# Gate/up products in another Strassen order with three PSUM copies, wide weight sums, and W_down sums one pair later

## The chip, the cores and the metric

The kernel runs on one core of a Trainium2 chip. The metric is the device time of one execution in microseconds (us); lower is better. Times are medians of several executions. A profile of one execution gives the span from the first to the last instruction, about 1.7 us shorter than the time. Runs are compared in the fast state only (granted TensorE clock near 1.00). Engines: PE is TensorE, PEld its weight loads, DVE VectorE, ACT ScalarE, POOL GpSimd, SP the engine whose queue issues the DMA transfers.

## The reference, cut to what matters

A transformer block on x of 2048 x 1024: linear attention (part A), then a gated MLP (part B). The change lies in part B.

```python
h  = x + _A_ref(_layernorm(x), A_wqkv, A_wo)
h2 = h + _B_ref(_layernorm(h), B_W_gate, B_W_up, B_W_down)

def _B_ref(x, W_gate, W_up, W_down):          # W_gate, W_up: 1024 x 3584, W_down: 3584 x 1024
    gate = x @ W_gate
    up   = x @ W_up
    gate = gate * (gate > 0)                  # ReLU
    return (gate * up) @ W_down
```

## The kernel before

Tokens go in two passes of 1024. In each pass 14 *pairs* compute gate and up for two blocks of 128 features, and then a down stage multiplies by W_down. All these products use a Strassen-Winograd scheme: seven products P1 to P7 in place of eight. It needs sums of weight blocks (T1 to T4), sums of activation blocks (S1 to S4, once a pass), sums of W_down blocks (once, in pass 0, kept in DRAM), and combinations of the products:

```text
U1 = P1+P6   C11 = P1+P2   C12 = U1+P5+P3   C22 = U1+P7+P5   C21 = U1+P7+P4 (signs inside the sums)
```

Each engine executes its own list in order. A helper turns the buffers that an operation reads and writes into semaphore waits, so an operation that waits for its data holds everything behind it on that engine:

```python
def emit(self, e, eng):
    for op in self.prog[e]:          # program order
        waits = {}                   # ... semaphores of the operations it depends on ...
        ins = op.fn(eng)
        ins._wait_ge(last[0], last[1])
```

One pair before the change (w = 0 is gate, w = 1 is up; BA, BF_, BB, BC_ are two PSUM banks each; `fillin(n)` puts n T sums for the next pair into the DVE list; `mid` are the W_down sums):

```python
for w in range(2):
    prod(w, BA[w], w_blk(w, 0, 0), a_blk(0, 0), True, "P1")
    ident_act(bank(BB[w]), bank(BA[w]), ..., "fk1")           # ACT: PSUM -> PSUM
fillin(2)
for w in range(2):
    prod(w, BF_[w], t_blk(w, 2), s_blk(2), True, "P7")
    ident_act(ftmp[:, w, :], bank(BF_[w]), ..., "s7")
fillin(2)
for w in range(2):
    prod(w, BB[w], t_blk(w, 1), s_blk(1), False, "P6")
    ident_act(bank(BC_[w]), bank(BB[w]), ..., "fk2")
fillin(2)
for f_ in mid:
    f_()                                                      # DVE: W_down sums
for w in range(2):
    prod(w, BA[w], w_blk(w, 1, 0), a_blk(1, 0), False, "P2")
    ...                                                       # rl11 on ACT after gate
# DVE: hh11 = BA[1] * r11
fillin(2)
for w in range(2):
    prod(w, BC_[w], t_blk(w, 0), s_blk(0), False, "P5")
    ident_act(ftmp[:, 2 + w, :], bank(BC_[w]), ..., "sc")
    # DVE: c22 = BF_[w] + ftmp[2 + w]
for w in range(2):
    prod(w, BB[w], t_blk(w, 3), a_blk(1, 1), False, "P4")
    # DVE: c21 = BB[w] + ftmp[w];  after gate also hh22 = max(c22 gate, 0) * c22 up
for w in range(2):
    prod(w, BC_[w], w_blk(w, 1, 1), s_blk(3), False, "P3")
    # after gate: rl12 on ACT, hh21 on DVE
# DVE: hh12 = BC_[1] * r12
load_w_next(); load_w_next()
```

One W_down pair's sums are four DVE subtractions that first need 512 KB of W_down:

```python
def wd_sums(q):
    add(0, wb(0, 1), wb(0, 0), [B_wraw[k]])       # waits until W_down of pair q has landed
    add(2, wb(1, 1), wb(0, 1), [B_wraw[k]])
    add(1, wb(1, 1), wsum[:, k, 0, :], ...)
    add(3, wb(1, 0), wsum[:, k, 1, :], ...)
    ...                                           # next load, store of the sums
```

And around the pairs:

```python
load_w_next()                                     # gate and up weights, 512 KB each
load_w_next()
for q in range(NWR):
    load_wraw(q)                                  # W_down, 512 KB each
wt_at = {0: [0], 1: [1, 2], 2: [3, 4]}            # pair -> W_down sums in it
for q in range(3, 12):
    wt_at[q] = [q + 2]
```

## Time and profile before

| what | value |
|---|---|
| time | 747.1 us (745.5 to 748.2, four runs) |
| span in the profile | 744.1 us |
| busy: PE, DVE, ACT | 98%, 72%, 42% |
| granted clock | 1.00 |

From the page of the kernel before: busy us by engine (share of the span, instructions), then the shares of the chain of work that ended last.

```profile
PE 731.3 (98%) x3914; PEld 330.4 (44%) x3975; DVE 534.4 (72%) x1064; ACT 316.2 (42%) x558; POOL 42.4 (6%) x93
...
PE 85%; DVE 7%; issue 3%; DMA 2%; ACT 2%; SPq 1%; POOL 0%; DVEq 0%; ACTq 0%
```

A matmul of 512 columns is shown as busy 379 ns, but matmuls overlap, so "98% busy" does not say that PE runs at its rate. Counting does. The view by windows gives busy us and, in brackets, instructions of each engine in stretches of time:

```profile
core 0: us, PE busy (x) PEld busy (x) DVE busy (x) ACT busy (x) POOL busy (x), PEclk, DMA share, GB/s
244.00:250.00 6.00, 5.27 (x23) 1.77 (x22) 5.93 (x12) 2.05 (x5) 0.00 (x0) 1.00 0.81 242
250.00:262.00 12.00, 11.95 (x56) 5.48 (x56) 11.76 (x28) 5.95 (x12) 0.00 (x0) 1.00 0.78 235
...
520.00:532.00 12.00, 11.95 (x56) 5.47 (x56) 8.63 (x19) 5.82 (x11) 0.00 (x0) 1.00 0.33 89
```

A pair has 56 matmuls, and 56 in 12 us is one per 0.214 us: that is the rate. From 244 to 250 us only 22 or 23 started where 28 would fit: PE waited there. DVE is nearly full in the early pairs (11.76 of 12 us) and has over a quarter of its time free in a late one (8.63).

The rate shows best in the start times of the weight loads, since there is one per matmul: the median spacing is 0.216 us. After 231 us only four spacings in the whole trace are over 0.26 us, all between 244.7 and 249.2 us. The first pair of pass 0 (pair 0) has its loads from 231.22 to 243.3 us.

The timeline of the kernel before around there (start, duration, engine, line, operation, output<-input, count; in brackets idle time just before and what ended it). L581 are the W_down sums, L1161 T sums, L1230 hh11, L1237 c22:

```profile
234.53 0.71 SPq L501 DMA_DIRECT2D RWG<-in_B_W_up_dram  x1
...
235.35 9.20 SPq L501 DMA_DIRECT2D RW<-in_B_W_down_dram  x3
...
237.56 0.76 DVE L1161 TENSOR_TENSOR RO<-RWG 128x512 f16<-128x512 bf16 x2 [1.84 <-DMA RWG<-in_B_W_up_dram]
...
242.55 1.56 DVE L581 TENSOR_TENSOR RW<-RW 128x512 f16<-128x512 bf16 x4 [4.23 <-issue]
...
244.03 0.68 DVE L1230 TENSOR_TENSOR RAB<-ps,RAB 128x512 bf16<-128x512 f32 x1
...
244.77 1.04 PE L595 MATMUL ps<-RH,RWG 128*128 128x512 bf16 x4 [0.22 <-DVE RAB L1230]
...
246.16 2.85 PE L595 MATMUL ps<-RC,RO 128*128 128x512 f16 x12 [0.35 <-DVE RE L1237]
```

DVE stood still for 4.23 us in front of the W_down sums, until 242.55. "issue" only says that the profile recorded no event that ended the wait. The view of the transfers into RW between 228 and 246 us fills this in:

```profile
DMA to landing us min/median/max: 3.9/5.7/7.1
```

The longest of these took 7.1 us. It was the first W_down request, of 235.35 us: the landing events kept in the packed trace put its landing at 242.47 us, 0.08 us before the sums began. hh11 started at 244.03, 7.4 us after the first matmul of P2 (236.61). Below, "lost in pair 0" means what the late DVE work of pair 0 cost, also where PE met it only in pair 1.

### The profile page before, as it was taken

How to read it: one execution, taken by the hardware profiler on the slowest of the kernel's cores; microseconds unless marked ns; L12 is line 12 of the kernel's file. 1: busy time of each engine (PE TensorE's matmuls, PEld its weight loads, DVE VectorE, ACT ScalarE, POOL GpSimd, SP SyncE). 2: the span in 40 equal slices, each digit the busy share in tenths (PEclk: the TensorE clock that was granted, in tenths of full speed). 3: DMA queues.
4: the chain of work that ended last, by engine and by line, in shares of the span. 5: the costliest groups of instructions: out<-in, count | busy, mean ns of one | idle time of the engine just before them, and what ended most of it. 6: DMA issues, size and time to landing. Idle time of an engine off the chain costs nothing.

```text
span 744.1 us, 10780 instructions
## 1 busy us (share of the span) xinstructions
PE 731.3 (98%) x3914; PEld 330.4 (44%) x3975; DVE 534.4 (72%) x1064; ACT 316.2 (42%) x558; POOL 42.4 (6%) x93
## 2 busy tenths in 40 slices
PE   8999999999999999999999999999999999999998
PEld 3444444344444444444444444444444444444443
DVE  7978877798775999787876495766767767563343
ACT  4887667764922354454543100045445454520000
POOL 1311100001350000000000010000000000000000
PEclk9999999999999999999999999999999999999999
DMA  9644144024999787555528899742424242036664
GB/s 314 195 102 70 32 139 156 1 30 87 216 225 286 223 258 222 171 169 170 142 87 261 225 286 280 246 118 69 113 57 113 58 114 56 1 86 185 211 193 133
DMA packets 160228, 113.43 MB, mean 152 GB/s; under 512 B 51504, under 2 KB 141360, under 8 KB 160176
## 3 DMA queue, kind: packets, MB, share of 16 engines
q1 hardware_dynamic: 159504, 112.09, 54.8%
q8 instruction: 31, 0.51, 0.3%
q10 hardware_dynamic: 672, 0.66, 0.3%
q14 instruction: 21, 0.17, 0.1%
HBM read 85.46 MB, written 15.73 MB: 136 GB/s over the span
## 4 chain that ended last, share of the span: by engine, by line
PE 85%; DVE 7%; issue 3%; DMA 2%; ACT 2%; SPq 1%; POOL 0%; DVEq 0%; ACTq 0%
PE ps L595 85%; SPq L501 1%; DVE RAB L681 1%; DMA RE<-in_A_x_dram 1%; DVE RE L1056 1%; DVE RX L678 1%; DMA RAB<-RXH 1%; DVE RX L897 1%; ACT RX L674 1%; ACT RXH L633 0%; DVE RWG L816 0%; DMA RW<-in_B_W_down_dram 0%; DVE RW L791 0%; ACT ps L600 0%; DVE RXH L1080 0%
## 5 line engine op out<-in xcount | busy, mean ns | idle before, releaser
L600 ACT ACTIVATE ps<-ps 128x512 f32<-128x512 f32 x156 | 90.8, 583 | 169.8 <-PE ps L595 151.2
L595 PE MATMUL ps<-RC,RO 128*128 128x512 f16 x672 | 154.4, 379 | 0.5 <-DVE RE L1237 0.4
L595 PE MATMUL ps<-RW,RAB 128*128 128x512 f16 (+1 forms) x686 | 151.3, 379 | 0.5
L595 PE MATMUL ps<-RH,RWG 128*128 128x512 bf16 x448 | 106.0, 379 | 0.2 <-DVE RAB L1230 0.2
L595 PEld LDWEIGHTS ps<-RW,RAB 128*128 128x128 bf16 (+1 forms) x696 | 68.1, 98 | 82.1
L600 ACT ACTIVATE RE<-ps 128x512 f32<-128x512 f32 x120 | 70.8, 597 | 75.3 <-PE ps L595 52.8
L595 PEld LDWEIGHTS ps<-RC,RO 128*128 128x128 f16 x672 | 65.5, 98 | 80.5 <-ACT ps L600 1.1
L595 PE MATMUL ps<-RC,RWG 128*128 128x512 f16 x320 | 76.8, 379 | 0.4 <-ACT ps L600 0.4
L595 PEld LDWEIGHTS ps<-RH,RWG 128*128 128x128 bf16 x448 | 43.8, 98 | 53.3 <-DVE RAB L1230 0.7
L1230 DVE TENSOR_TENSOR RAB<-ps,RAB 128x512 bf16<-128x512 f32 x28 | 19.3, 690 | 63.5 <-PE ps L595 63.5
L600 ACT ACTIVATE RAB<-ps 128x512 bf16<-128x512 f32 x56 | 33.4, 597 | 61.9 <-PE ps L595 61.8
L595 PE MATMUL ps<-RW,RE 128*128 128x512 bf16 x243 | 56.6, 380 | 1.6 <-DVE RXH L1080 0.7
L595 PE MATMUL ps<-RH,RO 128*128 128x512 bf16 (+1 forms) x228 | 55.5, 379 | 1.5
L595 PEld LDWEIGHTS ps<-RC,RWG 128*128 128x128 bf16 (+1 forms) x320 | 30.0, 98 | 40.2 <-ACT ps L600 6.2
L1161 DVE TENSOR_TENSOR RO<-RWG,RO 128x512 f16<-128x512 bf16 x108 | 45.4, 421 | 1.8
L1161 DVE TENSOR_TENSOR RO<-RWG 128x512 f16<-128x512 bf16 x108 | 40.7, 418 | 3.1 <-DMA RWG<-in_B_W_up_dram 1.8
L595 PE MATMUL ps<-RAB 128*128 128x512 bf16 x172 | 42.5, 379 | 0.3
L1237 DVE TENSOR_TENSOR RE<-ps,RE 128x512 f32<-128x512 f32 x56 | 38.3, 690 | 4.8 <-ACT RE L600 4.8
L1242 DVE TENSOR_TENSOR RE<-ps,RE 128x512 f32<-128x512 f32 x56 | 38.2, 682 | 0.0
L595 PEld LDWEIGHTS ps<-RH,RO 128*128 128x128 f16 (+1 forms) x256 | 24.4, 98 | 30.1 <-ACT RX L600 1.6
L595 PEld LDWEIGHTS ps<-RW,RE 128*128 128x128 bf16 x256 | 24.0, 98 | 28.8 <-DVE RXH L1080 1.2
L609 DVE BATCH_NORM_STATS2 st<-RE 128x6 f32<-128x512 bf16 x34 | 22.1, 683 | 16.4 <-DMA RE<-h_scr 12.5
(108 smaller groups left out, 756.0 us busy)
## 6 DMA issues: line engine op xcount, KB each, us to landing
RWG<-in_B_W_gate_dram SPq DMA_DIRECT2D x28, 512.0 KB, 4.1
RWG<-in_B_W_up_dram SPq DMA_DIRECT2D x28, 512.0 KB, 5.1
RW<-t_scr SPq DMA_DIRECT2D x56, 256.0 KB, 3.3
RW<-in_B_W_down_dram SPq DMA_DIRECT2D x42, 256.0 KB, 4.5
RW<-in_B_W_down_dram SPq DMA_DIRECT2D x14, 512.0 KB, 4.0
t_scr<-RW SPq DMA_DIRECT2D x14, 512.0 KB, 5.0
RE<-in_A_x_dram SPq DMA_DIRECT2D x23, 256.0 KB, 3.6
h_scr<-RXH SPq DMA_DIRECT2D x16, 256.0 KB, 3.4
```

The lines of the kernel that those rows point to most:

```text
L501: return PL.add(eng, lambda e: e.dma_start(dst_ap, src_ap), reads=reads, writes=writes, slot=slot, name=name)
L595: lambda e: e.matmul(out_ap, lhsT, rhs, start=start, stop=stop, skip_group_check=skip),
L600: PL.add("act", lambda e: e.activation(out=dst, in_=src, func=func), reads=reads, writes=writes, name=name)
L609: PL.add("dve", lambda e: e.bn_stats(out=st6[:, k, c * 6:(c + 1) * 6], in_=src_full[:, c * BCH:(c + 1) * BCH]), reads=[src_chunk_bufs[c]], ...
L674: PL.add("act", lambda e: e.activation(out=Et[:, k, :], in_=src, func=ACTF.Exp), reads=[src_buf], writes=[B_E[k]], name=name + "_exp")
L678: PL.add("dve", lambda e: e.tensor_scalar(out=Et[:, k, :], in0=Et[:, k, :], scalar1=1.0, scalar2=1e-6, op0=ALU.min, op1=ALU.add), reads=[] ...
L681: PL.add("dve", lambda e: e.scalar_tensor_tensor(out=dst_ap, in0=src, scalar=C1, in1=Et[:, k, :], op0=ALU.add, op1=ALU.max), reads=[src_bu ...
L897: PL.add("dve", lambda e: e.tensor_tensor(out=s_, in0=p_, in1=s_, op=ALU.add), reads=[pb], writes=[sb_], name=name + "_add")
L1161: PL.add(eng, lambda e: e.tensor_tensor(out=Tring[:, k, j], in0=in0, in1=in1, op=ALU.subtract), reads=reads, writes=[B_T[k][j]], name="T%d ...
L1230: PL.add("dve", lambda e: e.tensor_tensor(out=hh[:, f1, 0:SBW], in0=bank(BA[1]), in1=r11[:, rr, :], op=ALU.mult), reads=[B_bank[BA[1]], B_ ...
L1237: PL.add("dve", lambda e, w=w: e.tensor_tensor(out=ftmp[:, 4 + w, :], in0=bank(BF_[w]), in1=ftmp[:, 2 + w, :], op=ALU.add), reads=[B_bank[ ...
L1242: PL.add("dve", lambda e, w=w: e.tensor_tensor(out=ftmp[:, 6 + w, :], in0=bank(BB[w]), in1=ftmp[:, w, :], op=ALU.add), reads=[B_bank[BB[w] ...
```

## The change

Its intent: less DVE work per pair, no early stop of DVE. There are three parts.

1. The order becomes P1 P5 P6 P2 P7 P3 P4. P5 is copied once to SBUF (s5) and added in on DVE for both c22 and c12; U1+P7 stays in one bank and P4 is added on top of it. Three PSUM copies by ACT per matrix (fk1, s5, fk2) replace four; two Relus come in. c22 and c12 are bf16, so two of the four last products read SBUF only.
2. A T sum is made for gate and up in one operation of 128x1024 (POOL's first ones stay narrow).
3. The W_down sums start in pair 1.

(The order in which the T sums and the S sums are made changes a little, too; the cut below leaves that out.)

```diff
             for w in range(2):
                 prod(w, BA[w], w_blk(w, 0, 0), a_blk(0, 0), True, "P1")
                 ident_act(bank(BB[w]), bank(BA[w]), [B_bank[BA[w]]], [B_bank[BB[w]]], "fk1")
-            fillin(2)
+            fillin(1)
             for w in range(2):
-                prod(w, BF_[w], t_blk(w, 2), s_blk(2), True, "P7")
-                ident_act(ftmp[:, w, :], bank(BF_[w]), [B_bank[BF_[w]]], [B_s7[w]], "s7")
-            fillin(2)
+                prod(w, BE[w], t_blk(w, 0), s_blk(0), True, "P5")
+                ident_act(ftmp[:, w, :], bank(BE[w]), [B_bank[BE[w]]], [B_s5[w]], "s5")
+            fillin(1)
   ... P6 with fk2, mid, P2 with rl11, hh11 as before ...
             for w in range(2):
-                prod(w, BC_[w], t_blk(w, 0), s_blk(0), False, "P5")
-                ... sc copy, c22 add, then P4 with the c21 add, then P3 ...
+                prod(w, BB[w], t_blk(w, 2), s_blk(2), False, "P7")
+                add_s5(c22[:, w, :], bank(BB[w]), B_bank[BB[w]], w, B_c22[w], "c22")
+            relu(c22[:, 0, :], c22[:, 0, :], [], B_c22[0], "rl22")
+            for w in range(2):
+                prod(w, BC_[w], w_blk(w, 1, 1), s_blk(3), False, "P3")
+                add_s5(c12[:, w, :], bank(BC_[w]), B_bank[BC_[w]], w, B_c12[w], "c12")
+                if w == 0:
+                    mul(hh[:, f2, SBW:2 * SBW], c22[:, 0, :], c22[:, 1, :], B_c22, B_hh[f2][1], "hh22")
+            relu(c12[:, 0, :], c12[:, 0, :], [], B_c12[0], "rl12")
             for w in range(2):
                 prod(w, BB[w], t_blk(w, 3), a_blk(1, 1), False, "P4")
+                if w == 0:
+                    relu(r12[:, rr, :], bank(BB[0]), [B_bank[BB[0]]], B_r12[rr], "rl21")
+            mul(... c12 gate, c12 up ..., "hh12")
+            mul(... bank(BB[1]), r12 ..., "hh21")
   ... t_sums: the same subtractions with one more dimension, gate and up ...
-        wt_at = {0: [0], 1: [1, 2], 2: [3, 4]}
-        for q in range(3, 12):
+        wt_at = {1: [0, 1], 2: [2, 3], 3: [4, 5]}
+        for q in range(4, 12):
             wt_at[q] = [q + 2]
```

More of the change, by code (lines that the diff above doesn't have):

```diff
@@ L268, in bass_sequential_preLN__linear_attn_block__glu_gated_reglu__prompt_kernel @@
         ftmp = RE[:, 0:(NO + NOT) * D].bitcast(f32).rearrange("p (a b) -> p a b", b=SBW)
+        c22 = RE[:, 2 * D:4 * D].rearrange("p (a b) -> p a b", b=D)[:, :, 0:SBW]
+        c12 = RE[:, 4 * D:6 * D].rearrange("p (a b) -> p a b", b=D)[:, :, 0:SBW]
         o0 = (NO + NOT) * D
@@ L402, in bass_sequential_preLN__linear_attn_block__glu_gated_reglu__prompt_kernel @@
         B_f = bufs("f_", 8)
-        B_s7, B_sc, B_c22, B_c21 = B_f[0:2], B_f[2:4], B_f[4:6], B_f[6:8]
+        B_s5, B_c22, B_c12 = B_f[0:2], B_f[2:4], B_f[4:6]
         B_U, B_V = B_f[0:4], B_f[4:8]
@@ L1146, in s_sums @@
             return [
-                lambda: add(2, blk(0, 0), blk(0, 1), ALU.subtract, bl(0) + bl(1)),
                 lambda: add(0, blk(0, 1), blk(1, 1), ALU.add, bl(1)),
                 lambda: add(1, Ssum[:, 0], blk(0, 0), ALU.subtract, [B_S[0]] + bl(0)),
+                lambda: add(2, blk(0, 0), blk(0, 1), ALU.subtract, bl(0) + bl(1)),
                 lambda: add(3, blk(1, 0), Ssum[:, 1], ALU.subtract, [B_S[1]] + bl(0)),
@@ L1155, in t_sums, with wb, tb, add @@
             k = L % NTR
-            def wb(kk, h):
-                return wring[:, i, kk * KH:(kk + 1) * KH, h * P:(h + 1) * P]
-            def add(j, in0, in1, reads):
-                PL.add(eng, lambda e: e.tensor_tensor(out=Tring[:, k, j], in0=in0, in1=in1, op=ALU.subtract),
-                       reads=reads, writes=[B_T[k][j]], name="T%d_%d" % (j + 1, L))
-            return [
-                lambda: add(0, wb(0, 1), wb(0, 0), [B_w[i]]),
-                lambda: add(2, wb(1, 1), wb(0, 1), [B_w[i]]),
-                lambda: add(1, wb(1, 1), Tring[:, k, 0], [B_w[i], B_T[k][0]]),
-                lambda: add(3, wb(1, 0), Tring[:, k, 1], [B_w[i], B_T[k][1]]),
-            ]
+            n = 1 if eng == "pool" else 2
+            def wb(kk, h, u):
+                return wring[:, i + u:i + u + n, kk * KH:(kk + 1) * KH, h * P:(h + 1) * P]
+            def tb(j, u):
+                return Tring[:, k + u:k + u + n, j]
+            def add(j, f0, f1, td):
+                def go(u):
+                    r = range(u, u + n)
+                    PL.add(eng, lambda e: e.tensor_tensor(out=tb(j, u), in0=f0(u), in1=f1(u), op=ALU.subtract),
+                           reads=[B_w[i + x] for x in r] + ([B_T[k + x][td] for x in r] if td is not None else []),
+                           writes=[B_T[k + x][j] for x in r], name="T%d_%d" % (j + 1, L))
+                return [lambda u=u: go(u) for u in range(0, 2, n)]
+            return (add(0, lambda u: wb(0, 1, u), lambda u: wb(0, 0, u), None) +
+                    add(1, lambda u: wb(1, 1, u), lambda u: tb(0, u), 0) +
+                    add(2, lambda u: wb(1, 1, u), lambda u: wb(0, 1, u), None) +
+                    add(3, lambda u: wb(1, 0, u), lambda u: tb(1, u), 1))
         def hh_sums(q):
@@ L1185, in strassen_pair @@
             kt = [l % NTR for l in L]
-            BA, BF_, BB, BC_ = [0, 1], [2, 3], [4, 5], [6, 7]
+            BA, BE, BB, BC_ = [0, 1], [2, 3], [4, 5], [6, 7]
             rr = q % 2
@@ L1210, in prod, with add_s5, mul, relu @@
                        "%s%s_%d_%d" % (name, "gu"[w], ps_, q), skip=True)
+            def add_s5(dst, src, bsrc, w, bdst, name):
+                PL.add("dve", lambda e: e.tensor_tensor(out=dst, in0=src, in1=ftmp[:, w, :], op=ALU.add),
+                       reads=[bsrc, B_s5[w]], writes=[bdst], name=name)
+            def mul(dst, a_, b_, reads, wr, name):
+                PL.add("dve", lambda e: e.tensor_tensor(out=dst, in0=a_, in1=b_, op=ALU.mult), reads=reads,
+                       writes=[wr], name=name)
+            def relu(dst, src, reads, wr, name):
+                ident_act(dst, src, reads, [wr], name, func=ACTF.Relu)
             for w in range(2):
@@ L1222, in strassen_pair @@
                 ident_act(bank(BC_[w]), bank(BB[w]), [B_bank[BB[w]]], [B_bank[BC_[w]]], "fk2")
-            fillin(2)
+            fillin(1)
             for f_ in mid:
@@ L1228, in strassen_pair @@
                 if w == 0:
-                    ident_act(r11[:, rr, :], bank(BA[0]), [B_bank[BA[0]]], [B_r11[rr]], "rl11", func=ACTF.Relu)
-            PL.add("dve", lambda e: e.tensor_tensor(out=hh[:, f1, 0:SBW], in0=bank(BA[1]), in1=r11[:, rr, :],
-                                                    op=ALU.mult),
-                   reads=[B_bank[BA[1]], B_r11[rr]], writes=[B_hh[f1][0]], name="hh11")
-            fillin(2)
-            for w in range(2):
-                prod(w, BC_[w], t_blk(w, 0), s_blk(0), False, "P5")
-                ident_act(ftmp[:, 2 + w, :], bank(BC_[w]), [B_bank[BC_[w]]], [B_sc[w]], "sc")
-                PL.add("dve", lambda e, w=w: e.tensor_tensor(out=ftmp[:, 4 + w, :], in0=bank(BF_[w]),
-                                                             in1=ftmp[:, 2 + w, :], op=ALU.add),
-                       reads=[B_bank[BF_[w]], B_sc[w]], writes=[B_c22[w]], name="c22")
+                    relu(r11[:, rr, :], bank(BA[0]), [B_bank[BA[0]]], B_r11[rr], "rl11")
@@ new lines, in strassen_pair @@
+            mul(hh[:, f1, 0:SBW], bank(BA[1]), r11[:, rr, :], [B_bank[BA[1]], B_r11[rr]], B_hh[f1][0], "hh11")
+            fillin(1)
+            for w in range(2):
+                prod(w, BB[w], t_blk(w, 2), s_blk(2), False, "P7")
[6 more added lines that the diff above has]
+                    mul(hh[:, f2, SBW:2 * SBW], c22[:, 0, :], c22[:, 1, :], B_c22, B_hh[f2][1], "hh22")
@@ L1240, in strassen_pair @@
+            relu(c12[:, 0, :], c12[:, 0, :], [], B_c12[0], "rl12")
             for w in range(2):
                 prod(w, BB[w], t_blk(w, 3), a_blk(1, 1), False, "P4")
-                PL.add("dve", lambda e, w=w: e.tensor_tensor(out=ftmp[:, 6 + w, :], in0=bank(BB[w]),
-                                                             in1=ftmp[:, w, :], op=ALU.add),
-                       reads=[B_bank[BB[w]], B_s7[w]], writes=[B_c21[w]], name="c21")
                 if w == 0:
-                    PL.add("dve", lambda e: e.scalar_tensor_tensor(
-                        out=hh[:, f2, SBW:2 * SBW], in0=ftmp[:, 4, :], scalar=0.0, in1=ftmp[:, 5, :],
-                        op0=ALU.max, op1=ALU.mult), reads=B_c22, writes=[B_hh[f2][1]], name="hh22")
@@ L1249, in strassen_pair @@
-            for w in range(2):
-                prod(w, BC_[w], w_blk(w, 1, 1), s_blk(3), False, "P3")
-                if w == 0:
-                    ident_act(r12[:, rr, :], bank(BC_[0]), [B_bank[BC_[0]]], [B_r12[rr]], "rl12", func=ACTF.Relu)
-                    PL.add("dve", lambda e: e.scalar_tensor_tensor(
-                        out=hh[:, f1, SBW:2 * SBW], in0=ftmp[:, 6, :], scalar=0.0, in1=ftmp[:, 7, :],
-                        op0=ALU.max, op1=ALU.mult), reads=B_c21, writes=[B_hh[f1][1]], name="hh21")
@@ L1256, in strassen_pair @@
-            PL.add("dve", lambda e: e.tensor_tensor(out=hh[:, f2, 0:SBW], in0=bank(BC_[1]), in1=r12[:, rr, :],
-                                                    op=ALU.mult),
-                   reads=[B_bank[BC_[1]], B_r12[rr]], writes=[B_hh[f2][0]], name="hh12")
+                    relu(r12[:, rr, :], bank(BB[0]), [B_bank[BB[0]]], B_r12[rr], "rl21")
+            mul(hh[:, f2, 0:SBW], c12[:, 0, :], c12[:, 1, :], B_c12, B_hh[f2][0], "hh12")
+            mul(hh[:, f1, SBW:2 * SBW], bank(BB[1]), r12[:, rr, :], [B_bank[BB[1]], B_r12[rr]], B_hh[f1][1], "hh21")
@@ L1560, in bass_sequential_preLN__linear_attn_block__glu_gated_reglu__prompt_kernel @@
         LAG = NOT
-        pool_t = t_sums(0, "pool") + t_sums(1, "pool")
+        pool_t = t_sums(0, "pool")
         for t in range(NE, NST + LAG + 1):
@@ L1590, in bass_sequential_preLN__linear_attn_block__glu_gated_reglu__prompt_kernel @@
                 if nxt < NPASS * NPAIR * 2:
-                    fill = fill + t_sums(nxt) + t_sums(nxt + 1)
+                    fill = fill + t_sums(nxt)
                 if q > 0:
```

## The prediction

> **What bounds the kernel.** TensorE. The page gives PE busy 98%; the 20 us windows are the better test: from 250 us to the end 92 to 94 matmuls start in each, one per 0.215 us, at granted clock 1.00. The Trainium skill ("VectorE: DVE Perf Modes", section on the TRN2 errata) gives 215 ns for a 512-column matmul; the trace agrees (median spacing of weight loads 0.216 us). So gate/up and down run at the matmul rate. A gate/up pair is 56 matmuls; the chain of waits shows pairs as unbroken 12.03 us pieces of PE. DVE (72%) and ACT (42%) hide under that: DVE is busy 8.6 to 10 of 12 us in an ordinary pair, 11.8 in the three pairs with two W_down sums.
>
> After 225 us the weight loads show only four gaps, all in the first gate/up pair: 0.60, 0.73, 0.29, 0.53 us at 244.8, 246.2, 248.0, 249.2, together 2.15 us. The timeline says why: DVE executes in order, and the W_down sums of pair 0 (L581) wait 4.2 us, until 242.55, for W_down, requested at 235.35. hh11, T sums and c22 stand behind them, and TensorE waits for the banks they read.
>
> **What the change does.**
> - Matmuls: same number, order P1 P5 P6 P2 P7 P3 P4. No PE time saved.
> - ACT: still ten 0.6 us ops per pair (sc copies go, two Relus come). Neutral.
> - DVE: eight T sums of 0.42 us become four of 128x1024 at about 0.69 us (other sums of that size here: 0.682 to 0.692): minus 0.6 us per pair. hh22 and hh12 become bf16 SBUF products, about 0.42 instead of 0.69 us: minus 0.5. Ordinary pair: about 9.7 to 8.6 us. With two W_down sums (3.1 us): 11.7 of 12.03.
> - W_down sums start in pair 1, when their data have long landed.
>
> **On the critical path.** Almost only the 2.15 us. The saved DVE time, about 31 us over 28 pairs, lies under a saturated TensorE and buys nothing. The wide T sums of pair 0 wait for gate and up together; up landed at 237.5. Then T1 to T3 end at 239.6, hh11 at 240.3, T4 at 241.0, the c22 adds at 241.7 and 242.4, and P4, which overwrites those banks, is due at 241.75 and 242.6: pair 0 just fits, or leaves some tenths of a us. Later c22 ends about 1.2 us before P4 needs its bank, and hh21 ends 0.8 us into the next pair, whose copy into that bank starts at 1.8. No new stall in steady state. The stages before 220 us (some 20 us of small PE gaps) are untouched.
>
> Estimate: minus 2.15 plus 0.3 left over, so 745.8 us, 0.25% faster. Range 744.3 to 747.5. Faster by over 2%: 0.5%; within 2%: 98.5%; slower: 1%.
>
> **What would show it.** Right: span near 742; gaps at 244 to 249 gone or below 0.5 us; DVE busy down by about 30 us, its share 67 to 68%; T sums x108 of about 690 ns; matmuls per 20 us unchanged; no idle before the W_down sums. Wrong: PE waits on DVE or ACT (c22, c12, Relu in place, fk1) repeated in each pair, pairs longer than 12.03 us in the chain; wide sums well above 0.7 us.
>
> **What would make it wrong.** A repeated wait I mis-ordered (0.1 us per pair would be 2.8 us); the three W_down pairs, where DVE has 0.3 us to spare, turning a late load into gaps of 1 to 2 us; a lower granted clock. A gain over 2% (15 us) has no source: TensorE's whole idle in these stages is 2.15 us.

## The result, and the profile after

The changed kernel took 744.52 us (744.17 to 744.85, four runs) against 747.1 us. The ratio is 0.997, 95% interval 0.9956 to 0.9984: within 2%, and a small real gain. Here and below a ratio is the mean time of one kernel's fast runs over that of the other's of the same rounds, so not quite the ratio of the medians quoted.

From the page of the changed kernel, the lines that answer to those above:

```profile
PE 731.5 (98%) x3914; PEld 331.3 (45%) x3975; DVE 514.0 (69%) x956; ACT 318.7 (43%) x558; POOL 42.1 (6%) x93
...
PE 88%; DVE 7%; ACT 2%; issue 2%; DMA 1%; POOL 1%; DVEq 0%; ACTq 0%
```

The same windows of the changed kernel:

```profile
244.00:250.00 6.00, 6.00 (x30) 2.74 (x28) 5.38 (x12) 3.66 (x7) 0.00 (x0) 1.00 0.56 144
250.00:262.00 12.00, 11.95 (x57) 5.40 (x56) 11.22 (x25) 5.98 (x10) 0.00 (x0) 1.00 0.85 264
...
520.00:532.00 12.00, 11.95 (x57) 5.40 (x57) 7.89 (x15) 5.98 (x10) 0.00 (x0) 1.00 0.32 90
```

The stretch from 244 to 250 us now holds its 28 weight loads. In the late pair PE does what it did before, while DVE has 0.74 us less to do. The chain in order of time, from 225 us, is PE alone, in pieces of 12.03 us (a pair's length) with 0.05 us "issue" between them. In pair 0 of before it ran over W_down and DVE (the first two lines below are of the kernel before, the rest of the changed one):

```profile
238.32 4.23 issue
242.55 1.11 DVE RW L581 x3
...
230.26 12.03 PE ps L597 x55
242.29 0.05 issue
242.35 12.03 PE ps L597 x55
```

The timeline of the changed kernel in pair 0 (L1169 T sums, L1225 products, L1221 c22 and c12, L583 W_down sums):

```profile
237.97 0.69 DVE L1169 TENSOR_TENSOR RO<-RWG 128x1024 f16<-128x1024 bf16 x1 [4.72 <-DMA RWG<-in_B_W_up_dram]
...
239.91 0.68 DVE L1225 TENSOR_TENSOR RAB<-ps,RAB 128x512 bf16<-128x512 f32 x1
...
241.11 1.88 DVE L1221 TENSOR_TENSOR RE<-ps,RE 128x512 bf16<-128x512 f32 x3
...
242.35 1.67 PE L597 MATMUL ps<-RH,RO 128*128 128x512 bf16 x7
...
248.23 3.02 DVE L583 TENSOR_TENSOR RW<-RW 128x512 f16<-128x512 bf16 x8
```

DVE still waits 4.72 us in pair 0, now for the up weights alone, and is done just in time: the first c22 add ends near 241.8 us and the weight load of P4, which adds to the bank that it reads, is at 241.92 (of its eight matmuls the trace holds seven, from 242.35). The W_down sums at 248.23 wait for nothing.

**How much PE time was lost.** A gap in the weight loads is not quite lost time: PE loads weights ahead of its matmuls (in pair 0 the first load starts at 231.22 us, the first matmul at 231.43), and after a stop this lead is gone (244.76 and 244.77), so each gap is about 0.2 us longer than the time lost. The whole loss is read by aligning the two traces by the number of the weight load (3975 in both) and following the difference of their start times. From load 1640, in pair 0, to the last, the changed kernel takes 503.75 us. The kernel before takes 505.10: 1.34 us more, all in the first products of pair 1. The same measure of every fast trace follows; the column of loads 1560 to 1640 is a stretch at the end of the attention stage and the start of pair 0, where the kernels differ little (the order of some sums and loads):

```text
kernel          load 1640 to last   lost in pair 0*  lost in loads 1560-1640   lost later
before               505.10              1.34                0.00                0.00
before_again         505.45              1.70                0.90                0.00
changed              503.75              0.00                0.00                0.00
after_again          503.76              0.00                0.00                0.00
wd_late              503.75              0.00                0.00                0.00
wd_late_again        503.75              0.00                0.50                0.00
wd_load_first        503.76              0.00                0.00                0.00
wd_early             510.95              7.19                0.00                0.00
dve_double           504.94              1.19                0.00                0.00
lag_old              503.76              0.00                0.00                0.00
lag_new              505.82              0.00                1.05                2.06
after_slack          503.75              0.00                0.73                0.00
```

("lost" is against the trace of the changed kernel. * In the two traces of the kernel before it fell in pair 1, see above; in the others in P4 of pair 0.) Five hundred microseconds at 0.216 us per load leave nothing to gain after 235 us at this rate: no trace here took less than 503.75 us for this number of matmuls.

### The profile page after: what moved, and what is told of

The parts are those of the page before. It is cut to its first block, busy times and chain, and to the rows that moved or that the text cites. A ratio compares the mean times of both kernels' runs of the same rounds, so it can differ in the third digit from the quotient of the medians.

```text
span 743.1 us, 10650 instructions
## 1 busy us (share of the span) xinstructions
PE 731.5 (98%) x3914; PEld 331.3 (45%) x3975; DVE 514.0 (69%) x956; ACT 318.7 (43%) x558; POOL 42.1 (6%) x93
## 4 chain that ended last, share of the span: by engine, by line
PE 88%; DVE 7%; ACT 2%; issue 2%; DMA 1%; POOL 1%; DVEq 0%; ACTq 0%
PE ps L597 88%; DVE RAB L683 1%; ACT RX L676 1%; DVE RE L1058 1%; DMA RAB<-RXH 1%; DVE st L611 1%; DVE RX L680 1%; DVE RX L899 1%; POOL rstd L621 0%; DVE RW L793 0%; ACT ps L602 0%; DVE RXH L665 0%; DVE RC L793 0%; DMA RE<-in_A_x_dram 0%; DVE RWG L818 0%
## 5 line engine op out<-in xcount | busy, mean ns | idle before, releaser
L1225 DVE TENSOR_TENSOR RAB<-ps,RAB 128x512 bf16<-128x512 f32 x56 | 38.7, 692 | 87.7 <-PE ps L597 87.7
L1221 DVE TENSOR_TENSOR RE<-ps,RE 128x512 bf16<-128x512 f32 x112 | 74.4, 686 | 1.2 <-PE ps L597 0.3
L602 ACT ACTIVATE RE<-RE 128x512 bf16<-128x512 bf16 x56 | 35.3, 630 | 83.5 <-DVE RE L1221 83.5
L602 ACT ACTIVATE RE<-ps 128x512 f32<-128x512 f32 x64 | 37.6, 598 | 36.0 <-PE ps L597 35.7
L1169 DVE TENSOR_TENSOR RO<-RWG 128x1024 f16<-128x1024 bf16 x54 | 37.0, 684 | 4.7 <-DMA RWG<-in_B_W_up_dram 4.7
L1169 DVE TENSOR_TENSOR RO<-RWG,RO 128x1024 f16<-128x1024 bf16 x54 | 37.1, 687 | 1.0
```

The source lines that it names most:

```text
L602: PL.add("act", lambda e: e.activation(out=dst, in_=src, func=func), reads=reads, writes=writes, name=name)
L1169: PL.add(eng, lambda e: e.tensor_tensor(out=tb(j, u), in0=f0(u), in1=f1(u), op=ALU.subtract), reads=[B_w[i + x] for x in r] + ([B_T[k + x] ...
L1221: PL.add("dve", lambda e: e.tensor_tensor(out=dst, in0=src, in1=ftmp[:, w, :], op=ALU.add), reads=[bsrc, B_s5[w]], writes=[bdst], name=name)
L1225: PL.add("dve", lambda e: e.tensor_tensor(out=dst, in0=a_, in1=b_, op=ALU.mult), reads=reads, writes=[wr], name=name)
```

## The experiments

**Theory A**: the gain is the end of the stop in pair 0, and that stop came from the landing of W_down; DVE time saved elsewhere lies under PE. **Rival B**: the shorter DVE work and the new order make the gain. All outputs are right. The kernel before was timed again: 746.61, 746.42 and 746.36 us.

### The kernel before, a second trace (before_again)

> The kernel before, unchanged, to have a second trace of it. Theory A (the stall of pair 0 is set by the landing of W_down, which varies with the DMA traffic): the four gaps in the weight loads of pair 0 come again, and the matmul after them is between 1.0 and 3 us late against an unbroken rhythm (1.34 us in the first trace). If they are the same within 0.1 us, the landing does not vary and the spread of the timed runs of the kernel before (745.5 to 748.2) is elsewhere. Time 747 us.

746.36 us (ratio 0.9995, interval 0.9983 to 1.0008). The four gaps came again, 0.95, 0.73, 0.28 and 0.54 us; lost in pair 0: 1.70 us, 0.36 more than in the first trace. Its sums waited again:

```profile
243.83 1.56 DVE L581 TENSOR_TENSOR RW<-RW 128x512 f16<-128x512 bf16 x4 [4.38 <-issue]
```

The landing events of the two traces explain the difference: the first W_down landed 11.04 us after the pair's first matmul in the first trace (242.47 against 231.43) and 11.39 us after it in this one (243.75 against 232.36), 0.35 us later. So the stop varies with the landing, as theory A says. But the end of the attention stage varies, too: 0.90 us were lost there in this trace and none in the first, and three other traces of the table, of both orders, lost 0.50 to 1.05 us there.

### The W_down sums moved alone (wd_late)

```diff
-        wt_at = {0: [0], 1: [1, 2], 2: [3, 4]}
-        for q in range(3, 12):
+        wt_at = {1: [0, 1], 2: [2, 3], 3: [4, 5]}
+        for q in range(4, 12):
             wt_at[q] = [q + 2]
```

(in the kernel before)

> The kernel before with the W_down sums moved alone (pairs 1, 2, 3 take two each, pair 0 none). Theory A (the late start of the W_down sums is the whole gain): no gaps in pair 0, time equal to the changed kernel within 0.1%, about 744.5 to 745. Rival B (the narrower DVE work of wide sums and new order is needed, too): DVE has about 12.2 to 12.8 us of work in pairs 1 to 3 against 12.03 us, its lag grows by up to 0.7 us a pair and new gaps of up to 1 us in all appear in pairs 2 to 4; time 745.5 to 746.5.

744.48 us, ratio 0.9976 (0.9963 to 0.9988), no gap after 231 us. In its trace hh11 waits for nothing but its own product, and in the next stretch DVE has room for two W_down sums:

```profile
238.59 0.69 DVE L1230 TENSOR_TENSOR RAB<-ps,RAB 128x512 bf16<-128x512 f32 x1 [0.23 <-PE ps L595]
...
243.30:255.40 12.10, 12.05 (x57) 5.46 (x57) 11.60 (x27) 5.92 (x11) 0.00 (x0) 1.00 0.74 223
```

W_down's first piece landed 11.10 us after the pair's first matmul here, as late as in the kernel before (11.04), and cost nothing. This one edit gives the whole gain. Rival B's gaps in pairs 2 to 4 did not come: in those pairs DVE was busy 11.6 of 12.1 us. I had added up durations, and back-to-back DVE operations overlap a little (see below).

### The changed kernel without that part (wd_early)

The same edit backwards, in the changed kernel.

> The changed kernel with the old place of the W_down sums (pair 0 takes one). Theory A: the stall of pair 0 is back, the sums wait about 4 us for W_down, gaps of 1.3 to 2 us in TensorE; time 1.3 to 2.5 us above the changed kernel, about 746 to 747, equal to the kernel before. Rival B (order and wide sums give the gain): stays at 744.5 to 745.

751.32 us, ratio 1.0060 (1.0047 to 1.0074). The direction was theory A's, the size three times what I expected: the new order and wide sums with early W_down sums are 4.7 us slower than the kernel before. Its timeline:

```profile
239.16 0.69 DVE L1169 TENSOR_TENSOR RO<-RWG 128x1024 f16<-128x1024 bf16 x1 [5.53 <-DMA RWG<-in_B_W_up_dram]
...
244.16 1.56 DVE L583 TENSOR_TENSOR RW<-RW 128x512 f16<-128x512 bf16 x4 [2.98 <-issue]
...
246.83 1.88 DVE L1221 TENSOR_TENSOR RE<-ps,RE 128x512 bf16<-128x512 f32 x3
...
247.97 3.19 PE L597 MATMUL ps<-RH,RO 128*128 128x512 bf16 x7 [5.31 <-DVE RE L1221]
247.97 0.15 PEld L597 LDWEIGHTS ps<-RH,RO 128*128 128x128 f16 x1 [0.28 <-issue]
248.40 0.15 PEld L597 LDWEIGHTS ps<-RH,RO 128*128 128x128 f16 x1 [0.28 <-issue]
```

DVE was 0.9 us later than in the kernel before, counted from the start of pair 0 (W_down sums at 244.16 here and 242.55 there, pair 0 from 232.14 and 231.43). Measured against its own order without the early sums, hh11 was late by nearly the same time in both: 5.4 us in the kernel before (against wd_late), 5.35 us here (13.49 us after the pair's first matmul, 8.14 in the changed kernel). But the old order lost 1.3 to 1.7 us by it, and this one 7.2. In the old order the first bank that PE needs back from a late DVE is that of hh11, in the next pair. In the new order it is that of c22, because P4 of the *same* pair adds to it: PE stopped for 5.3 us at P4. In the changed kernel pair 0 had no time to spare there (c22 ended 0.13 us before P4's load), so nearly all of the lateness became a stop. The wide sums alone don't cost this: in wide_only, below, they stand in the old order with the early W_down sums and lose nothing. The new order with narrow sums was not run, so the share of each in the 7.2 us is not separated.

The rest, some 2 us, is the clock. After the stop ten loads come some 0.43 us apart, and the windows of this run show the granted clock (third figure from the end):

```profile
232.00:242.00 10.00, 10.00 (x48) 4.53 (x47) 3.21 (x4) 4.12 (x7) 0.00 (x0) 1.00 0.97 268
242.00:247.90 5.90, 0.66 (x4) 0.23 (x3) 3.71 (x8) 0.35 (x1) 0.00 (x0) 0.76 0.51 149
247.90:251.80 3.90, 3.83 (x9) 1.36 (x9) 2.70 (x6) 1.51 (x3) 0.00 (x0) 0.50 1.06 350
251.80:260.00 8.20, 8.20 (x39) 3.76 (x38) 7.18 (x17) 4.12 (x7) 0.00 (x0) 1.00 0.53 149
```

The Trainium skill ("TensorE: Matmul & The Clock Gate", "What's actually happening") says that the clock falls to half after at least one idle window of about 3.4 us and returns after about as long a time of work. This trace agrees in the main: a stop of 5.3 us, then half clock. The time differs a little, and there the measurement decides. A mean of 0.76 over the second window means that the clock fell at about 245.05 us, 3.0 us after the last weight load before the stop (242.07), so sooner than 3.4 us of standing still. It was full again from 251.88 us, 4.3 us after the first load that followed the stop (247.57). The stops of under 1 us in the kernel before left the clock at 1.00.

### Wide T sums alone (wide_only)

The new `t_sums` in the kernel before; the order and the place of the W_down sums stay.

```diff
-            fillin(2)
+            fillin(1)
...
-                    fill = fill + t_sums(nxt) + t_sums(nxt + 1)
+                    fill = fill + t_sums(nxt)
```

> The kernel before with the wide T sums alone. Theory A: DVE busy falls by about 15 to 17 us (0.6 us in each of 27 pairs), the four gaps in pair 0 stay or grow by some tenths (the wide sums also wait for the later of the two weight loads); time as before within 0.2%, 746.5 to 748. Rival B: a gain of 1 us or more.

746.39 us, ratio 0.9999 (0.9986 to 1.0013), over the four fast runs (746.0 to 746.8). No gain, against rival B. The profiled run fell in the slow state (853.91 us, granted clock 0.851), so its trace is used for nothing but operation lengths: the 108 wide sums took 684 to 687 ns on average, 74.1 us, where the narrow ones took 86.1. That is 12 us saved, not the 15 to 17 of my expectation, which had counted 0.6 us a pair; it is 0.44.

### The W_down loads first (wd_load_first)

```diff
-        load_w_next()
-        load_w_next()
         for q in range(NWR):
             load_wraw(q)
+        load_w_next()
+        load_w_next()
```

(in the kernel before; the W_down sums stay in pair 0)

> The kernel before, its W_down sums still in pair 0, but the two first W_down loads put ahead of the gate and up loads of pair 2 in the queue. Theory A (the landing of W_down holds DVE, not the place of the sums): W_down is requested about 1.5 us earlier and lands 2 to 3 us earlier, the sums start near 240 us, hh11 ends before the next pair's P1 needs its bank (about 244.2), no gap is left; time as the changed kernel, 744.5 to 745.3. Rival (the sums in pair 0 are too much work at that place): gaps of 1 us or more stay, time 746 to 747.

744.9 us, ratio 0.9982 (0.9969 to 0.9994), no gap after 222 us. In its timeline the request is early, the wait short and hh11 (L1230) early enough:

```profile
234.54 1.15 SPq L501 DMA_DIRECT2D RW<-in_B_W_down_dram  x2
...
239.90 1.55 DVE L581 TENSOR_TENSOR RW<-RW 128x512 f16<-128x512 bf16 x4 [0.75 <-issue]
...
241.38 0.68 DVE L1230 TENSOR_TENSOR RAB<-ps,RAB 128x512 bf16<-128x512 f32 x1
```

So what held DVE was the landing of W_down behind 1 MB of weights that nobody needed yet, not the place of the sums or their amount. This settles what "issue" hid.

### More DVE work under PE (dve_double)

In the changed kernel every wide T sum of pass 1 is done twice.

```diff
-                    fill = fill + t_sums(nxt)
+                    ts = t_sums(nxt)
+                    fill = fill + ([f_ for f_ in ts for _ in range(2)] if p_ == 1 else ts)
...
-            fillin(1)
+            fillin(1 + ps_)
```

> The changed kernel with each wide T sum of pass 1 done twice: 13 pairs with four more operations of 0.61 to 0.69 us, 32 to 36 us more DVE work in all, more than the change saved. Theory A (DVE time in ordinary pairs is hidden under TensorE): no gap in TensorE, time within 0.1% of the changed kernel, 744.3 to 745. Rival C (DVE time saved is worth part of the gain): 1 us or more longer.

745.03 us, ratio to the kernel before 0.9980 (0.9967 to 0.9993). In pass 1, from 520 to 532 us, DVE was busy 10.54 us, against 7.89 in the changed kernel and 8.63 before, and PE did its pair:

```profile
520.00:532.00 12.00, 12.00 (x57) 5.47 (x56) 10.54 (x19) 5.86 (x10) 0.00 (x0) 1.00 0.33 89
```

No PE time was lost in pass 1: more DVE time was put in there (548.8 us busy in all, against 514.0) than the change had taken out (534.4 before), at no cost. But 1.19 us were lost in pair 0, which this edit doesn't touch:

```profile
239.24 0.69 DVE L1169 TENSOR_TENSOR RO<-RWG 128x1024 f16<-128x1024 bf16 x1 [6.18 <-DMA RWG<-in_B_W_up_dram]
...
243.12 1.90 PE L597 MATMUL ps<-RH,RO 128*128 128x512 bf16 x8 [1.01 <-DVE RE L1221]
```

Here the up weights came 7.66 us after the pair's first matmul (231.58), against 6.20 us in the first trace of the changed kernel: the narrow fit that the prediction had named, missed by a late landing.

### The reserve of the two orders (lag_new, lag_old)

Sixteen spare DVE additions stand before hh11 in pairs 3, 6 and 9 of pass 1, once in the changed kernel (lag_new) and once in wd_late (lag_old).

```diff
+        def lag(n):
+            for x in range(n):
+                i = x % NOS
+                PL.add("dve", lambda e, i=i: e.tensor_tensor(out=outst[:, i, :], in0=hnT[:, 0, 0:NW],
+                                                             in1=hnT[:, 1, 0:NW], op=ALU.add), ...)
...
+                if p_ == 1 and q in (3, 6, 9):
+                    mid.append(lambda: lag(16))
                 strassen_pair(p_, q, fill, mid)
```

> The changed kernel with 16 spare DVE additions (about 6.0 us together) before hh11 in three pairs of pass 1. Reading from its trace: DVE idles 3.37 us before hh11, and the first c22 add ends 1.5 us before P4 needs its bank, so 4.9 us of lag are free and the rest stops TensorE: about 1.1 us in each of the three pairs, 3.3 us in all, first at P4; time about 748. Rival (both orders bear the same lag): no gap, as lag_old.

> The old product order (kernel before with late W_down sums) with the same 16 spare DVE additions in the same three pairs. Reading from its trace: 3.06 us of idle before hh11, and the first consumer (copy into the bank of c21 and the next P6) comes 3.9 us after, so 6.9 us of lag are free: no gap in TensorE; time as wd_late, 744.5 to 745. Rival: 1 us per pair, as lag_new.

lag_new took 746.7 us and lost 0.69 us in each of the three pairs, 2.06 in all (and 1.05 us at the end of the attention stage in its profiled run). lag_old took 744.43 us and lost nothing. lag_new in the second of its pairs:

```profile
563.94 5.45 DVE L1597 TENSOR_TENSOR RX<-RH 128x512 bf16<-128x512 bf16 x16
...
569.31 0.69 DVE L1225 TENSOR_TENSOR RAB<-ps,RAB 128x512 bf16<-128x512 f32 x1
...
570.51 1.88 DVE L1221 TENSOR_TENSOR RE<-ps,RE 128x512 bf16<-128x512 f32 x3
...
571.25 1.90 PE L597 MATMUL ps<-RH,RO 128*128 128x512 bf16 x8 [0.52 <-DVE RE L1221]
```

The additions held DVE for 5.37 us (563.94 to 569.31), not 6.0, so the loss was smaller than expected. The new order bears 5.37 less 0.69, about 4.7 us of DVE lag before hh11; the old order bears at least 5.4 us, though its DVE has more work. That it bears 6.9, as I read from its trace, was not tried.

### Pair 0 without the dependence, and a head-to-head (after_again, after_slack, wd_late_again)

**Theory D**: the changed kernel loses up to 1.5 us in pair 0 in some executions, by late up weights. **Rival E**: the loss in dve_double came from its doubled sums. In after_slack the T sums of pair 0 come after the c12 adds and after hh21:

```diff
-            def fillin(n):
-                for _ in range(n):
+            def fillin(n, late=False):
+                for _ in range(n if late or Lg else 0):
...
+            if Lg == 0:
+                fillin(2, late=True)       # after rl12, and again after hh21
```

> The changed kernel, unchanged, again, beside the kernels of this call. Theory D (its pair 0 fits only when the up weights of pair 2's slot, the fourth load, land less than about 6.5 us after the pair's first matmul; they landed 6.2 us after it in the first trace, 7.7 us in that of dve_double, which has the same pair 0 and lost 1.2 us there): the loss in pair 0 is between 0 and 1.5 us from run to run, time 744.2 to 745.8. Rival E (the loss of dve_double came from its doubled sums): no gap in pair 0 in this trace and time 744.5.

> The changed kernel with the wide T sums of pair 0 moved behind its c12 adds and its last product, so that hh11 and c22 don't stand behind a landing of weights. Theory D: no gap in pair 0 whenever the weights land, time as the old order with late W_down sums, and 0 to 0.6 us below the changed kernel of the same call, about 744.3. Rival E: equal to the changed kernel within 0.1 us. Risk: T1 ends 0.2 us before P5 of pair 1 needs it, so a new gap of some tenths may stand there.

> The old order with the late W_down sums again, beside the changed kernel: theory A says the two are equal within 0.1% (0.7 us), with no gap in pair 0, as it bears some 5 us of lag there; theory D adds that its runs spread no more than the changed kernel's. Time 744.4.

They took 744.87, 744.89 and 744.80 us; ratios to the kernel before 0.9977, 0.9977 and 0.9980. None lost time in pair 0 in its profiled run; in after_again the up weights came 6.25 us after the pair's first matmul. So the three are equal within the noise, and after_slack gained nothing, where theory D had allowed up to 0.6 us. Theory D's forecast that wd_late_again would spread no more was not borne out either (744.1 to 746.1 us, after_again 743.5 to 745.4). Four traces have the changed kernel's pair 0 as it is (changed, after_again, dve_double, lag_new) and one of them shows a loss; in wd_early, which has the same loads, the up weights came late as well (7.02 us), hidden there behind the wait for W_down. The trace of dve_double shows the late landing and the wait behind it before any doubled sum runs, so rival E has no mechanism left; but how often it happens is open, and its mean cost is too small to be seen in these times. No version beat the changed kernel clearly; the simplest equal is wd_late, a two-line edit.

## Why the prediction was right

- *Forecast.* 745.8 us (744.3 to 747.5) against 744.52 measured, and 744.87 when repeated. Within 2% at 98.5%: right.
- *PE bounds the kernel and its only idle time in these stages is in pair 0.* Right, except for the place: the gaps lie in P1, P7 and P6 of pair 1, the second pair, as PE ran on until it needed the banks that pair 0's DVE work still held. All gap-free kernels take the same 503.75 us from load 1640 on, whatever their order and their DVE load.
- *The cause, W_down sums that wait on an in-order DVE.* Right, and shown by three runs: moved alone (wd_late, 0.9976), put back (wd_early, 1.0060), landing earlier (wd_load_first, 0.9982). The two traces of the kernel before agree: a landing 0.35 us later, a loss 0.36 us larger.
- *2.15 us on the critical path.* A mis-sized term. It added up gaps in the weight loads, and each overstates the loss by 0.2 us. Aligned traces give 1.34 us, and 1.70 in a second trace.
- *0.3 us left over in pair 0.* Right in kind: nothing in three traces, 1.19 us in dve_double.
- *The sum.* I forecast minus 1.8 us; the medians differ by 2.6 and by 1.5, and wd_late by 2.1. The two traces explain 1.3 to 1.7 us. That the forecast came so near is partly luck: a saving counted some 0.8 us too high and 0.3 us of leftover that these traces don't show cancel in part. What may remain is no larger than the spread of single runs, to which the end of the attention stage gives up to 1 us.
- *DVE saves about 31 us.* As a sum of durations it is 28.8: the T, c and hh groups were 239.5 us and are 210.7. The page's DVE busy time fell by only 20.4 us (534.4 to 514.0), and its share to 69%, not 67 to 68. The step that failed is adding durations: operations of 0.69 us start every 0.60 to 0.61 us when they follow each other (241.18 and 241.78 us in dve_double), and busy time counts an overlap once.
- *Wide sums of about 690 ns; hh22 and hh12 about 0.42.* Measured: 684 and 687 ns, and 420 ns. The Trainium skill ("VectorE: DVE Perf Modes", "The perf-mode tier table") allows tensor_tensor double rate in bf16 from SBUF and single rate from PSUM; here a product took 692 ns with a PSUM operand and 420 without, which agrees in direction (1.65 times, and not double).
- *No new stall in steady state.* Right. What the prediction didn't see is the price: P4 in the same bank as c22 shortens what PE bears of a late DVE, from at least 5.4 to 4.7 us in the pairs of pass 1 that were tried and to almost nothing in pair 0, where a late W_down cost 7.2 us (wd_early) in place of 1.3 to 1.7. The first two parts of the change need the third.

## What to carry to other kernels

Where the bounding engine already starts its operations at its full rate, time saved on another engine was worth nothing by itself here; look for the few places where its rhythm breaks, and for the operation at the head of an in-order queue that waits there, and first try to move that one operation or its load alone. Before making a helper engine's list shorter by sharing a buffer, count how late that engine may be before the main engine needs the buffer back: less work and less reserve can come together. Measure lost time by aligning two traces by operation number, not by adding up gaps.

## What the Trainium skill lacked or had wrong

- "Perfetto Trace Analysis" ("Identifying the Most-Contended Engine") rightly distrusts matmul busy time and offers the busy share of weight loads. Here that was 44% and 45% for a rhythm with a gap and one without, and no more than 45% (5.40 of 12 us) in a stretch at the full rate: it did not show the loss. The spacing of the loads did, with a catch that no page has: each gap overstates the lost time by about 0.2 us (2.15 us of gaps, 1.34 us lost).
- "TensorE: Matmul & The Clock Gate" ("What's actually happening") was useful: 5.3 us of stop, then half clock and ten loads some 0.43 us apart, which cost about 2 us on top of the stop. It asks for at least one idle window of about 3.4 us before the fall. In wd_early the clock fell 3.0 us after the last weight load, so the 3.4 us before the fall were not all idle.
